# Keeping the numbers of a 1/rms iteration in free PSUM columns instead of in SBUF

## The chip, the cores and the metric

The kernel runs on one core of one Trainium2 chip. The metric is the device time of one execution in microseconds; 17 small VectorE instructions in each of four places are what changes.

## The reference, cut to what matters

The reference is an attention over 32 memory slots, followed by a gated feed-forward layer with an RMS norm in front (8 batches, 8 heads, 576 positions, head dimension 64, model width 512, inner width 1536, all fp32):

```python
x = attn_out.transpose(0, 2, 1, 3).reshape(B * S, H * D)   # 4608 x 512
rms = np.sqrt(np.mean(x * x, axis=-1, keepdims=True) + 1e-06)
xn = x / rms * rms_g
g = xn @ w_gate
silu = g * (1.0 / (1.0 + np.exp(-g)))
val = xn @ w_val
return (silu * val @ w_out).astype(np.float32)
```

The change concerns 1/rms alone: one number for each of the 4608 rows of x.

## The kernel before, in words

The batches are worked in four pairs, numbered 0 to 3. A pair has 1152 rows of x, held as 128 partitions by NT = 9 columns of row groups, so 1/rms of a pair is one tile of 128 x 9 floats, `rinv`. x itself is never formed: the kernel keeps the attention weights `a` and multiplies the weight matrices by the batch's memory values, and the sum of squares of a row is the weights times a Gram matrix times the weights again.

`x_steps` makes the steps for a pair. `turn` (line 184) transposes the attention weights on TensorE into `tp`, and `copy` (line 194) takes them to SBUF as `at`. `mm` (line 235) multiplies `at` by the Gram matrix `gb` into a PSUM tile `xp`, one for each of the nine groups; only its first 256 of 512 columns are used. `square` (line 248) multiplies `xp` by the weights and adds up each row into `ssq`. `fin` (lines 258 to 278) then computes 1/sqrt by a bit trick and four rounds of three instructions on VectorE: 17 instructions on 128 x 9 numbers, nearly all of which depend on the one before. `spread` transposes `rinv` on TensorE (`rp`, line 204), multiplies `at` by it on VectorE (line 212), and splits the product into a high and a low part: `ath` on ScalarE (line 223) and `atl` on GpSimd (line 224). The products of the feed-forward layer (lines 840, 876, 918) read these.

Pairs 0 and 1 pass through this in the first stage, together with the reductions of k and v (line 573 and its followers 588, 596, 597, 599, 605, 617, 642), the scores of the attention (lines 706, 717, 719, 726, 737 to 746) and the conversion of the weights from doubles in lines 345 to 403. There the PSUM tiles of `xp` come from a ring of two banks named "kx", which `kvp` and `kvt` use too. Pairs 2 and 3 pass through it in the second stage, beside the feed-forward products of pairs 0 and 1. There `xp`, the transposes and the output products `po` (line 918) share a ring of two banks named "o"; `po` is added to `acc` on VectorE (line 925), which frees its bank. Line 854 subtracts there the high part of a product from it, line 885 multiplies the two halves of the gate.

The order of the instructions is written out: every step has a date in a list (`ev`) from the constants in `PRM`, the list is sorted, and the steps are issued in that order; a scheduler then places each engine's instructions in a fixed order, by that priority and its own estimate of time, and gives out the banks of a ring. On the chip each engine works through its list and waits where an input or a bank isn't ready. Input transfers go through one queue, SP's.

Of the kernel before, what the change touches and what calls it, by code (L numbers as in the profile page):

```python
# [8 lines left out]
F32 = mybir.dt.float32  # L9
F32R = mybir.dt.float32r  # L10
I32 = mybir.dt.int32
U32 = mybir.dt.uint32
AF = mybir.ActivationFunctionType
ALU = mybir.AluOpType
# [76 lines left out]
def kernel(  # L91
# [25 lines left out]
    nc = tc.nc  # L117
    P = 128
# [3 lines left out]
    NT = S // 64  # L122
    NP = B // 2
    DM = H * D
# [7 lines left out]
    persist = ctx.enter_context(tc.tile_pool(name="persist", bufs=1))  # L132
# [9 lines left out]
    rinv = [persist.tile([P, NT], F32, name=f"rinv{i}") for i in range(NP)]  # L142
# [4 lines left out]
    ssqs = {}  # L147
# [14 lines left out]

    def x_steps(pr, a, psum_t, psum_x, fetch=None):

        tps, xps, srcs, st = {}, {}, {}, {}
        i = pr % G

        def first():
# [61 lines left out]
        def mm(t):  # L230
            def f():
                xps[t] = xp = psum_x(f"xp{pr}_{t}")
                for cc in range(2):
                    for j in range(2):
                        nc.tensor.matmul(  # L235
                            xp[64 * j:64 * j + 64, P * cc:P * cc + P],
                            st["at"][:, t, cc, 64 * j:64 * j + 64],
                            gb[:, j, cc],
                            start=True, stop=True,
                        )  # L240
            return f
# [13 lines left out]
            return f  # L255

        def fin():
            m = persist.tile([P, NT], F32, tag="m", name=f"m{pr}")
            nc.vector.tensor_scalar(
                out=m, in0=ssqs[pr], scalar1=0.0, scalar2=1.0 / DM, op0=ALU.max, op1=ALU.mult  # L260
            )
            nc.vector.tensor_scalar_add(m, m, 1e-6)
            r = rinv[pr]
            ri = r.bitcast(I32)
            nc.vector.tensor_scalar(
                out=ri, in0=m.bitcast(I32), scalar1=1, scalar2=None, op0=ALU.logical_shift_right
            )
            nc.vector.tensor_scalar(
                out=ri, in0=ri, scalar1=-1.0, scalar2=float(0x5F3759DF), op0=ALU.mult, op1=ALU.add
            )  # L270
            nc.vector.tensor_scalar(out=m, in0=m, scalar1=-0.5, scalar2=None, op0=ALU.mult)
            u = persist.tile([P, NT], F32, tag="u", name=f"u{pr}")
            for _ in range(4):
                nc.vector.tensor_tensor(out=u, in0=r, in1=r, op=ALU.mult)
                nc.vector.tensor_tensor(out=u, in0=u, in1=m, op=ALU.mult)
                nc.vector.scalar_tensor_tensor(
                    out=r, in0=u, scalar=1.5, in1=r, op0=ALU.add, op1=ALU.mult
                )
        events = [(-0.1, first)]
        for t in range(NT):  # L280
# [3 lines left out]
            if fetch and t % 4 == 0:  # L284
                events.append((t / 100 - 0.05, fetch(t)))
        p = NT + PRM["LAG"]
        events.append((p, fin))
        for t0, n in ((0, 4), (4, 4), (8, 1)):
            events += zip((p + PRM["RO"], p + PRM["RO"] + PRM["RS"], p + PRM["RO"] + 2 * PRM["RS"]), spread(t0, n))
# [138 lines left out]
    with ExitStack() as c1:  # L428
# [31 lines left out]
        st = {}  # L460
# [293 lines left out]
        def tile_of(tag):  # L754
            return lambda name: ps.tile([P, 512], F32, tag=tag, name=name, bufs=PRM["B"][0 if tag == "tr" else 1])
# [35 lines left out]
        for pr in range(G):  # L791
            for s in range(HP):
                t = PRM["S_AT"][pr * HP + s]
                steps = q_steps(pr, s)
                ev.append((t - PRM["QL"] - PRM["OL"] - PRM["QD"][pr * HP + s], lambda pr=pr, s=s: load_q(pr, s)))
                ev.append((t - PRM["QL"] - PRM["OL"], steps[0]))
                ev += place(t - PRM["QL"], PRM["QO"], steps[1:])
                ev += place(t, PRM["SO"], score_steps(pr, s))
            if pr < G:
                ev += [(PRM["X_AT"][pr] + PRM["XP"] * p, f) for p, f in x_steps(  # L800
                    pr, lambda t, pr=pr: a_tiles[pr][:, t], tile_of("tr"), tile_of("kx"))]
# [16 lines left out]
    def where(i):  # L818

        ps_, r = divmod(i, NU * G * 2)  # L820
        u, r = divmod(r, G * 2)
        pi, f = divmod(r, 2)
        return ps_, u, ps_ * G + pi, 2 * u + f
# [197 lines left out]
    def x2(pr):  # L1021
        got = {}

        def fetch(t):
            def f():
                for tag, t0, n in (("qr", 0, 4), ("qT", 4, 4), ("ex", 8, 1)):
                    if t0 == t:
                        a = sb.tile([P, n, 256], F32, tag=tag, name=f"ain{pr}_{t0}")
                        nc.sync.dma_start(a, a_dram[pr][:, t0:t0 + n])
                        for k in range(n):  # L1030
                            got[t0 + k] = a[:, k]
            return f
        steps = x_steps(pr, got.pop, o_tile, o_tile, fetch)
        return [f for _, f in steps]
# [7 lines left out]
    for i in range(NS):  # L1042
        ps_, u, pr, j = where(i)
# [62 lines left out]
```

## Time and the profile before

| | us |
|---|---|
| median of 3 runs | 908.46 (908.34 to 909.11) |
| the profiled execution | 907.8 |
| its span from first to last instruction | 906.0 |
| TensorE busy in matmuls | 837.0 (92%) |
| VectorE busy | 575.7 (64%) |
| ScalarE busy | 420.2 (46%) |
| GpSimd busy | 326.2 (36%) |

The page and the trace call the engines PE (TensorE matmul), PEld (TensorE weight load), DVE (VectorE), ACT (ScalarE), POOL (GpSimd) and SP (SyncE). L276 is line 276 of the kernel. `out<-in` names the tiles that an instruction writes and reads, then come partitions x elements and type. Idle time of an engine before an instruction stands behind it in square brackets, with what ended it. Shares over the whole span are averages of stages with different limits.

### The profile page before, as it was taken

Reading aid. Unit: us, or ns where it says so; the run is one execution under the profiler, and the core shown is the slowest. Engines: PE = TensorE matmul, PEld = TensorE weight load, DVE = VectorE, ACT = ScalarE, POOL = GpSimd, SP = SyncE. Lnnn points to the kernel's source line nnn. Section 1 sums busy time; section 2 is a strip of 40 time slices with the busy share of each in tenths; the row PEclk is TensorE's granted clock in tenths of the full one; section 3 lists DMA queues with packets and bytes.
Section 4 is the critical chain, followed back from the end, with each engine's and each line's share of the span. In section 5 each row is a group of like instructions: output and inputs, shape, how many; then the busy total and the mean of one; then the engine's idle time right before and its main releaser. Section 6 shows DMA issues by size and latency. Waiting matters only on the chain.

```text
span 906.0 us, 15847 instructions
## 1 busy us (share of the span) xinstructions
PE 837.0 (92%) x6207; PEld 744.5 (82%) x6207; DVE 575.7 (64%) x994; ACT 420.2 (46%) x717; POOL 326.2 (36%) x274
## 2 busy tenths in 40 slices
PE   4998485899998899999999999999999999999997
PEld 4776474788986798888898997799899999999996
DVE  5577959896788777877855656532445455454543
ACT  2666334787765355664642443254424333233330
POOL 3464735553636245344532331411212121121120
PEclk9899787999999999999999999999999999999999
DMA  8986554454445332543413133501204013040046
GB/s 277 337 278 209 201 166 120 168 146 107 164 133 162 101 119 84 152 114 103 140 57 129 52 88 118 121 31 47 94 1 140 1 47 93 1 140 1 1 114 142
DMA packets 81506, 106.41 MB, mean 117 GB/s; under 512 B 34324, under 2 KB 52248, under 8 KB 81432
## 3 DMA queue, kind: packets, MB, share of 16 engines
q1 hardware_dynamic: 81432, 105.41, 37.6%
q8 instruction: 49, 0.80, 0.4%
q14 instruction: 25, 0.20, 0.1%
HBM read 73.93 MB, written 31.46 MB: 116 GB/s over the span
## 4 chain that ended last, share of the span: by engine, by line
PE 73%; DVE 14%; DMA 4%; ACT 3%; issue 3%; POOL 2%; SPq 1%; POOLq 0%; ACTq 0%; DVEq 0%
PE po L918 30%; PE pv L876 15%; PE pg L876 15%; PE vp L840 7%; DMA phi<-in_phi_dram 2%; PE xp L235 2%; DVE mi L365 1%; DVE mi L369 1%; DVE xl L854 1%; DVE ex L345 1%; PE kvp L573 1%; DMA q<-in_q_dram 1%; DVE ex L347 1%; DVE acc L925 1%; SPq L298 1%
## 5 line engine op out<-in xcount | busy, mean ns | idle before, releaser
L899 POOL TENSOR_TENSOR hl<-hf,hh 128x512 fp32r<-128x512 f32 (+1 forms) x96 | 139.8, 1457 | 361.3 <-ACT hh L898 353.3
L925 DVE TENSOR_TENSOR acc<-po,acc 128x512 f32<-128x512 f32 x180 | 123.0, 687 | 128.0 <-PE po L918 127.2
L918 PE MATMUL po<-oh,hh 128*128 128x512 f32 x432 | 173.5, 403 | 8.3 <-DVE acc L925 5.2
L918 PE MATMUL po<-oh,hl 128*128 128x512 f32 x432 | 171.3, 397 | 0.0
L918 PE MATMUL po<-ol,hh 128*128 128x512 f32 x432 | 171.0, 396 | 0.0
L884 ACT ACTIVATE sg<-pg 128x256 f32<-128x256 f32 x192 | 78.2, 409 | 171.2 <-PE pg L876 150.0
L854 DVE TENSOR_TENSOR xl<-vp,xh 64x1024 fp32r<-64x1024 f32 x96 | 117.1, 1220 | 48.1 <-ACT xh L853 47.0
L885 DVE TENSOR_TENSOR hf<-pv,sg 128x256 f32<-128x256 f32 x192 | 85.5, 453 | 79.1 <-PE pv L876 51.6
L853 ACT CAST xh<-vp 64x1024 fp32r<-64x1024 f32 x96 | 96.6, 1007 | 53.6 <-PE vp L840 25.5
L918 PEld LDWEIGHTS po<-oh,hh 128*128 128x128 f32 x432 | 81.5, 189 | 23.5 <-DVE acc L925 7.5
L898 ACT CAST hh<-hf 128x512 fp32r<-128x512 f32 (+1 forms) x96 | 64.6, 673 | 77.0 <-DVE hf L885 54.2
L918 PEld LDWEIGHTS po<-oh,hl 128*128 128x128 f32 x432 | 81.4, 189 | 19.4
L876 PE MATMUL pg<-ath,xh 128*128 128x320 f32 (+1 forms) x384 | 86.6, 300 | 8.5 <-ACT xh L853 6.0
L918 PEld LDWEIGHTS po<-ol,hh 128*128 128x128 f32 x432 | 81.7, 189 | 11.1
L840 PE MATMUL vp<-wh,vm 128*128 128x256 f32 x384 | 86.9, 289 | 3.5 <-DVE at L212 2.3
L876 PE MATMUL pv<-ath,xh 128*128 128x320 f32 (+1 forms) x384 | 84.8, 300 | 3.2 <-DVE hf L885 3.1
L876 PE MATMUL pg<-atl,xh 128*128 128x320 f32 (+1 forms) x384 | 85.0, 297 | 0.0
L876 PE MATMUL pg<-ath,xl 128*128 128x320 f32 (+1 forms) x384 | 84.8, 295 | 0.0
L876 PE MATMUL pv<-atl,xh 128*128 128x320 f32 (+1 forms) x384 | 84.5, 297 | 0.0
L876 PE MATMUL pv<-ath,xl 128*128 128x320 f32 (+1 forms) x384 | 84.1, 297 | 0.0
L876 PEld LDWEIGHTS pg<-ath,xh 128*128 128x128 f32 x384 | 63.6, 191 | 14.1 <-ACT xh L853 6.6
L840 PEld LDWEIGHTS vp<-wh,vm 128*128 128x128 f32 x384 | 66.8, 193 | 6.2 <-DVE at L212 2.5
(129 smaller groups left out, 1394.6 us busy)
## 6 DMA issues: line engine op xcount, KB each, us to landing
kv<-in_k_dram SPq DMA_DIRECT2D x32, 288.0 KB, 5.0
kv<-in_v_dram SPq DMA_DIRECT2D x32, 288.0 KB, 5.6
out_dram<-acc SPq DMA_DIRECT2D x72, 128.0 KB, 2.4
raw<-in_moe_w_gate_dram SPq DMA_DIRECT2D x12, 512.0 KB, 3.9
raw<-in_moe_w_val_dram SPq DMA_DIRECT2D x12, 512.0 KB, 3.7
wd<-wh SPq DMA_DIRECT2D x12, 512.0 KB, 3.0
wd<-wl SPq DMA_DIRECT2D x12, 512.0 KB, 4.5
raw<-in_moe_w_out_dram SPq DMA_DIRECT2D x12, 512.0 KB, 3.5
```

The costliest lines, as they stand in the source:

```text
L235: nc.tensor.matmul(xp[64 * j:64 * j + 64, P * cc:P * cc + P], st["at"][:, t, cc, 64 * j:64 * j + 64], gb[:, j, cc], start=True, stop=True,)
L298: issued.append(nc.sync.dma_start(out, in_).ins)
L840: nc.tensor.matmul(vp[:, cc, e, :], lhs(l), r[:, 2 * cc + e, :], start=(n == 0), stop=(n == 2),)
L853: nc.scalar.copy(xh[rows], src)
L854: nc.vector.tensor_tensor(out=xl[rows], in0=src, in1=xh[rows].bitcast(F32), op=ALU.subtract)
L876: nc.tensor.matmul(pt[:, :N], l[:, cc, b, half * P:half * P + P], r[:, b, cc, t0:t0 + n, :].rearrange("p t x -> p (t x)"), start=(m == 0), ...
L884: nc.scalar.activation(sg[:, :N], pg[:, :N], AF.Silu)
L885: nc.vector.tensor_tensor(out=hf[:, :, b, :], in0=pv[:, :N].rearrange("p (t x) -> p t x", x=64), in1=sg[:, :N].rearrange("p (t x) -> p t x ...
L898: nc.scalar.copy(hh, hv)
L899: nc.gpsimd.tensor_tensor(out=hl, in0=hv, in1=hh.bitcast(F32), op=ALU.subtract)
L918: nc.tensor.matmul(po, l[:, tt, :], r, start=(m == 0), stop=(m == 5))
L925: nc.vector.tensor_tensor(out=accs[key], in0=po, in1=accs[key], op=ALU.add)
```

## The change

In `fin`, the numbers m and r of the iteration move from SBUF tiles into two stretches of nine columns (256 to 264 and 272 to 280) of the PSUM tile of the pair's last `xp`; m is written back to SBUF by the instruction that multiplies it by -0.5, u stays in SBUF, and the last instruction writes `rinv` in SBUF as before. The product that was r*r, then times m, is now r*m, then times r. The count of instructions is the same. The last `xp` is now used until the iteration's last instruction.

```diff
--- before.py
+++ after.py
@@ -162,7 +162,7 @@
 
     def x_steps(pr, a, psum_t, psum_x, fetch=None):
 
-        tps, xps, srcs, st = {}, {}, {}, {}
+        tps, xps, srcs, st, xlast = {}, {}, {}, {}, []
         i = pr % G
 
         def first():
@@ -230,6 +230,7 @@
         def mm(t):
             def f():
                 xps[t] = xp = psum_x(f"xp{pr}_{t}")
+                xlast[:] = [xp]
                 for cc in range(2):
                     for j in range(2):
                         nc.tensor.matmul(
@@ -255,26 +256,26 @@
             return f
 
         def fin():
-            m = persist.tile([P, NT], F32, tag="m", name=f"m{pr}")
+
+            mp, rp = (xlast[0][:, 256 + 16 * k:256 + 16 * k + NT] for k in range(2))
+            m, u = (persist.tile([P, NT], F32, tag=x, name=f"{x}{pr}") for x in "mu")
             nc.vector.tensor_scalar(
-                out=m, in0=ssqs[pr], scalar1=0.0, scalar2=1.0 / DM, op0=ALU.max, op1=ALU.mult
+                out=mp, in0=ssqs[pr], scalar1=0.0, scalar2=1.0 / DM, op0=ALU.max, op1=ALU.mult
             )
-            nc.vector.tensor_scalar_add(m, m, 1e-6)
-            r = rinv[pr]
-            ri = r.bitcast(I32)
+            nc.vector.tensor_scalar_add(mp, mp, 1e-6)
+            ri = rp.bitcast(I32)
             nc.vector.tensor_scalar(
-                out=ri, in0=m.bitcast(I32), scalar1=1, scalar2=None, op0=ALU.logical_shift_right
+                out=ri, in0=mp.bitcast(I32), scalar1=1, scalar2=None, op0=ALU.logical_shift_right
             )
             nc.vector.tensor_scalar(
                 out=ri, in0=ri, scalar1=-1.0, scalar2=float(0x5F3759DF), op0=ALU.mult, op1=ALU.add
             )
-            nc.vector.tensor_scalar(out=m, in0=m, scalar1=-0.5, scalar2=None, op0=ALU.mult)
-            u = persist.tile([P, NT], F32, tag="u", name=f"u{pr}")
-            for _ in range(4):
-                nc.vector.tensor_tensor(out=u, in0=r, in1=r, op=ALU.mult)
-                nc.vector.tensor_tensor(out=u, in0=u, in1=m, op=ALU.mult)
+            nc.vector.tensor_scalar(out=m, in0=mp, scalar1=-0.5, scalar2=None, op0=ALU.mult)
+            for k in range(4):
+                nc.vector.tensor_tensor(out=u, in0=rp, in1=m, op=ALU.mult)
+                nc.vector.tensor_tensor(out=u, in0=rp, in1=u, op=ALU.mult)
                 nc.vector.scalar_tensor_tensor(
-                    out=r, in0=u, scalar=1.5, in1=r, op0=ALU.add, op1=ALU.mult
+                    out=rinv[pr] if k == 3 else rp, in0=u, scalar=1.5, in1=rp, op0=ALU.add, op1=ALU.mult
                 )
         events = [(-0.1, first)]
         for t in range(NT):
```

## Rows read from the trace of the kernel before

**Rows 1.** Table of stages: us from:to, length, busy us and instructions of each engine, PEclk, DMA share, GB/s.
```profile
91.00:104.00 13.00, 6.86 (x135) 6.51 (x136) 12.63 (x32) 3.83 (x8) 8.23 (x11) 0.90 0.69 233
104.00:117.00 13.00, 7.95 (x75) 6.85 (x75) 12.58 (x23) 5.07 (x11) 10.01 (x10) 0.58 0.33 122
122.00:128.00 6.00, 4.93 (x40) 3.79 (x38) 0.98 (x4) 2.30 (x6) 3.20 (x4) 0.73 1.01 349
499.00:517.00 18.00, 18.00 (x115) 16.09 (x114) 11.42 (x31) 6.92 (x12) 3.86 (x3) 1.00 0.06 15
```

**Rows 2.** Waits from 85 to 155 us: who for whom, us in total, times, longest.
```profile
PE rp L204 <- DVE rinv L276: 7.6, 2, 5.6
```

**Rows 3.** Order of time on VectorE, pair 0: start us, us, engine, line, operation.
```profile
93.03 1.12 DVE L259 TENSOR_SCALAR m<-ssq 128x9 f32<-128x9 f32 x1
...
94.72 0.90 DVE L347 TENSOR_SCALAR ex<-ex 128x512 int32<-128x512 int32 x1
...
97.97 0.66 DVE L275 TENSOR_TENSOR u<-u,m 128x9 f32<-128x9 f32 x1
98.66 1.18 DVE L276 SCALAR_TENSOR_TENSOR rinv<-u,rinv 128x9 f32<-128x9 f32 x1
99.88 0.41 DVE L274 TENSOR_TENSOR u<-rinv 128x9 f32<-128x9 f32 x1
...
100.75 1.19 DVE L274 TENSOR_TENSOR u<-rinv 128x9 f32<-128x9 f32 x1
...
103.33 0.16 DVE L276 SCALAR_TENSOR_TENSOR rinv<-u,rinv 128x9 f32<-128x9 f32 x1
```

**Rows 4.** Order of time on GpSimd, beside pair 0.
```profile
94.08 1.26 POOL L403 TENSOR_TENSOR wl<-w,wh 128x512 fp32r<-128x512 f32 x1
97.77 0.83 POOL L737 TENSOR_TENSOR half<-ex 128x288 f32<-128x288 f32 x1 [2.42 <-DVE rinv L268]
98.56 1.25 POOL L385 TENSOR_TENSOR w<-mi,ex 128x512 f32<-128x512 f32 x1
...
100.65 1.26 POOL L403 TENSOR_TENSOR wl<-w,wh 128x512 fp32r<-128x512 f32 x1
```

**Rows 5.** Order of time on VectorE, pair 1.
```profile
136.25 0.17 DVE L259 TENSOR_SCALAR m<-ssq 128x9 f32<-128x9 f32 x1
...
138.11 1.23 DVE L276 SCALAR_TENSOR_TENSOR rinv<-u,rinv 128x9 f32<-128x9 f32 x1
```

**Rows 6.** Order of time on GpSimd, beside pair 1.
```profile
138.05 1.26 POOL L403 TENSOR_TENSOR wl<-w,wh 128x512 fp32r<-128x512 f32 x1 [10.94 <-PE kvp L573]
```

**Rows 7.** VectorE's groups by shape, 85 to 155 us: count, busy us, mean ns, idle before.
```profile
L248 DVE CUSTOM_DVE_ANT_0 xp<-xp,a 128x256 f32<-128x256 f32 x13 | 5.5, 435 | 4.5 <-PE xp L235 4.4
...
L719 DVE TENSOR_TENSOR ex<-S,mxs 128x576 f32<-128x576 f32 x3 | 2.3, 754 | 0.0
...
L605 DVE TENSOR_TENSOR kb<-kvp,im 128x256 f32<-128x256 f32 x3 | 1.2, 400 | 0.1
...
L597 DVE RECIPROCAL si<-si 128x2 f32<-128x2 f32 x3 | 0.5, 161 | 0.0
...
L596 DVE TENSOR_SCALAR si<-kvp 128x2 f32<-128x2 f32 x3 | 0.5, 154 | 1.6 <-PE kvp L588 1.6
```

**Rows 8.** The page's costliest groups: busy us, mean ns, idle before, releaser.
```profile
L925 DVE TENSOR_TENSOR acc<-po,acc 128x512 f32<-128x512 f32 x180 | 123.0, 687 | 128.0 <-PE po L918 127.2
...
L854 DVE TENSOR_TENSOR xl<-vp,xh 64x1024 fp32r<-64x1024 f32 x96 | 117.1, 1220 | 48.1 <-ACT xh L853 47.0
```

**Rows 9.** Order of time on TensorE, pair 3.
```profile
562.74 0.50 PE L918 MATMUL po<-oh,hh 128*128 128x512 f32 x1
...
564.25 0.39 PE L918 MATMUL po<-oh,hh 128*128 128x512 f32 x1
...
572.30 1.04 PE L204 MATMUL rp<-ident,rinv 128*128 128x128 f32 x4 [2.26 <-DVE rinv L276]
```

**Rows 10.** Order of time on VectorE, pair 3.
```profile
568.64 1.09 DVE L275 TENSOR_TENSOR u<-u,m 128x9 f32<-128x9 f32 x1
```

## The prediction

> **What bounds the kernel now.** I began with the table of stages: it shows which engine fills each stretch. From 91 to 117 us VectorE is the full one (12.63 of 13 us, then 12.58 of 13), while TensorE is busy for 6.86 and 7.95 us of it; from 499 to 517 us TensorE works 18.00 of 18.00 us [rows 1]. So the four runs of the iteration do not stand in the same surroundings. Pairs 0 and 1 (from 93 and 136 us [rows 3, 5]) lie where VectorE sets the pace, pairs 2 and 3 (after 500 and 560 us) lie beside TensorE work. The list of waits between 85 and 155 us confirms the first half: TensorE waits twice for line 276, the iteration's last line, 7.6 us together and 5.6 us the longer [rows 2]. I then read the order of time on VectorE through the iteration of pair 0, with GpSimd's beside it.
>
> There the reader is to see two things. A free instruction on nine columns takes 0.16 to 0.17 us, but in pair 0 some take 0.41 to 1.19 us [rows 3]. And the longest three of the dependent ones end where a GpSimd instruction ends: line 276, from 98.66 to 99.84, against GpSimd's line 385 until 99.82; line 274, from 100.75 to 101.94, against line 403 until 101.91; line 275, until 98.63, against line 737 until 98.56 [rows 3, 4]. They did not work, they waited for GpSimd. In pair 1 one instruction does the same: 138.11 to 139.34, while GpSimd's line 403 runs from 138.05 to 139.31 [rows 5, 6].
>
> Which instructions wait? The ones held in rows 3 and 5 read two SBUF operands, or are a tensor_scalar from SBUF to SBUF. Those with one operand in PSUM do not: line 248 (PSUM and SBUF in, PSUM out) means 435 ns over 13 instructions and line 719 means 754 ns over 3, in the same crowded stretch [rows 7]. That is the row on which the forecast stands.
>
> **The change, part by part.** The count stays: 17 VectorE instructions for each of four pairs, 68 in all. No transfer, matmul or ScalarE instruction is added. What differs is operands and how long one PSUM bank is held.
>
> *a. Two SBUF operands become one.* Lines 274 to 276 read rp from PSUM and one SBUF operand each. The first five work on mp and rp; only the first of them still reads SBUF. If they behave as line 248, the holds go.
> Pair 0, with 0.17 as the free duration [rows 3]: line 275 0.66 - 0.17 = 0.49; line 276 1.18 - 0.17 = 1.01; line 274 0.41 - 0.17 = 0.24 and 1.19 - 0.17 = 1.02. Sum 2.76 us. Line 259 took 1.12 too, but I count nothing for it: if it shrank, line 347 (tensor_scalar, SBUF) would come 0.95 earlier and sit out the same GpSimd instruction, which starts at 94.08 and lasts until 95.34; line 347 already ends only at 95.62 [rows 3, 4]. So 2.76 is the figure, with 0 below it, if later SBUF instructions take over the hold, and 3.7 above.
> Pair 1: 1.23 - 0.17 = 1.06 us [rows 5].
> Does it reach the end? After pair 0 VectorE stays full until 117, and its next instructions read PSUM (717, 719, 596, 212). I take all of it. The transfers that saturate from 122 to 128 us (DMA share 1.01) [rows 1] were issued only when that VectorE work let the queue go on, so they move along; the other view is a rival below. After pair 1 lines 212, 223 and 224 follow directly and the pairs' first products wait for them.
>
> *b. The price of a PSUM operand on nine columns.* The trace has no chain that writes PSUM and reads it back. Nearest rows: line 596 reads PSUM and takes 154 ns for 128x2, line 597 reads SBUF and takes 161 ns, so -7 ns; line 248 reads and writes PSUM, 435 ns, against 400 for line 605, which writes SBUF, so +35 ns [rows 7]. Bounds -0.1 to +0.6 us for 17 instructions. I take 0, since the durations of 596 and 597 are those of our size.
> [...]
>
> *c. Order inside the iteration.* Before, u = r*r needed only r; line 271 (m times -0.5) ran beside line 268. Now u = rp*m needs both, and both touch one bank. Consecutive dependent instructions start 0.21 us apart (9 such steps in 1.86 us from 136.25 to 138.11 [rows 5]), so at most one such step more, and about 0.1 if the two still overlap: I take +0.15 for each pair, 0.3 on the path for pairs 0 and 1 (bounds 0 and 0.42).
>
> *d. The bank of the last xp is held until the iteration ends.* In pairs 0 and 1 the ring is "kx" with two banks. After xp of pair 0 the next user takes the bank of the one before it, and the following one (line 617) needs line 605's output first, which comes after the iteration. The same order holds in pair 1. Cost 0, bounds 0 and about 0.5.
> In pairs 2 and 3 the ring is "o", two banks, through which the output products of line 918 pass. With one bank left, each waits for line 925 of the one before, 687 ns [rows 8], and its hand-over, about 0.9 us, unless other products stand between. Pair 2: most have others between; I count one short stall, 0.3 us (bounds 0 and 0.9). Pair 3: four such products run in a row from 562.74 us, 1.5 us each (the second starts at 564.25 [rows 9]), so three stalls, 2.7 us; but TensorE then idles 2.26 us at 572.30 for the iteration's result anyway [rows 9], and line 275 there loses its hold, 1.09 - 0.17 = 0.92 [rows 10]. If the VectorE order stays, the later 925s push the end of the iteration out by 2.7 - 0.92 = 1.8; if two of them move behind it, it ends 0.92 + 2 x 0.69 = 2.3 earlier, about the idle time that there is to win. I take 0 between them.
>
> **Sum.** -2.76 - 1.06 + 0.3 + 0.3 + 0 = -3.2 us. The profiled execution takes 907.8 (span 906.0, 1.8 around it), so 904.6; the median of the runs shown, 908.46, is 0.66 above that execution: 905.3 us.
>
> **Rivals.**
> 1. *The wait only moves.* GpSimd stays as busy, and a later SBUF instruction (lines 744, 345) takes over pair 0's hold, or the transfers before 128 us do not come earlier. For it: DMA share 1.01 from 122 to 128 [rows 1]. Against: only 0.33 before it, so that burst was late issued rather than a backlog. Left: pair 1's 1.06 less 0.15 and pair 2's 0.3: -0.6, 907.8 us.
> 2. *A PSUM operand costs.* At the upper bound of 35 ns [rows 7], 17 instructions cost 0.6 us in each of pairs 0, 1 and 3: -3.2 + 1.8 = -1.4, 907.1 us. It eats all at about 0.1 us an instruction in pairs 0 and 1 (3.2 / 34). [...]
> 3. *The held bank blocks the output products (slower).* If the next user of the "o" ring is bound to the held bank instead of the free one, the second product after the last xp waits until the iteration ends. Pair 2: at least 3.6 us (the iteration takes 17 x 0.21 = 3.6). Pair 3: 3.6 plus an interleaved line 854, 1.2 us, and line 925, 0.7 [rows 8], 5.5, less the idle 2.26: 3.3. Together 6.9 against the gain of 3.8 - 0.3: +3.4, 911.9 us. It decides from stalls of 3.5 us on. For it: TensorE has no slack at 499 to 517 [rows 1]. Against: each ring has a free bank at that moment, and there are other products to put there.
> 4. *The change doesn't act:* the holds stay although an operand is in PSUM: 908.5. Line 248 and 719 speak against it; small.
>
> **How the numbers follow.** Forecast 0.53; rival 1 0.15, rival 2 0.14, rival 3 0.14, rival 4 0.04. A measurement of this kernel tells about 0.2% from no change, 1.8 us, so same is 906.6 to 910.3. The forecast's own range, from the bounds of a to d and pair 3's -2.3 to +1.8, is 902.4 to 907.4; about a tenth of it is inside "same". Rivals 1, 2 and 4 lie in "same" (a quarter of rival 2 is faster); rival 3 is slower in most of its span, and a changed order of work adds a little to slower. Faster 0.55, same 0.28, slower 0.17. Leaving out rival 3 and the far ends, 8 in 10 lie between 902.4 and 909.0.
>
> **What the profile after would show.** Step a: no instruction of the iteration over 0.25 us in pairs 0 and 1 (line 259 perhaps), and TensorE's 5.6 us wait for line 276 near 2.9. Step b: free durations within 0.03 of 0.17, starts 0.21 apart. Step c: line 271 a step after 268. Step d: TensorE's idle time before line 918 under 1 us at 500 to 517, and its idle time before line 204 in pair 3 below 2.26. Also the first products of line 876, after 154 us, some 3.5 us earlier. Wrong would be: starts over 0.3 apart (rival 2), line 918 waiting for line 276 (rival 3), the same date of the first line 876 products (rival 1), or another order of instructions that moves the whole middle of the kernel.

## The result and the profile after

The changed kernel takes 912.8 us (median of 6 runs, 910.21 to 914.93), the kernel before 908.4 beside it: ratio 1.005, 95% interval 1.003 to 1.0069. That is 4.5 us slower (0.005 x 908.4), where 3.2 us faster was forecast. A second series of the same program, in the experiments below, gave 1.0036 (1.0019 to 1.0054), 3.3 us. Both intervals lie above 1; the two figures, 4.5 and 3.3 us, are each known to about 1.7 us either way.

Where the time goes is not where the change is. The iteration itself did what the forecast said. This is the order of time of the profile after, on VectorE and then on GpSimd, through pair 0; it answers to [rows 3, 4]. In the changed file the iteration stands in lines 262 to 277; every line from 233 on has moved down by one or more.

```profile
92.79 0.15 DVE L262 TENSOR_SCALAR xp<-ssq 128x9 f32<-128x9 f32 x1
...
93.52 0.64 DVE L348 TENSOR_SCALAR ex<-ex 128x512 int32<-128x512 int32 x1
94.08 1.77 DVE L370 SCALAR_TENSOR_TENSOR mi<-raw,mi 128x512 f32<-128x512 uint32 x1
...
97.38 0.17 DVE L273 TENSOR_SCALAR m<-xp 128x9 f32<-128x9 f32 x1
97.58 0.17 DVE L275 TENSOR_TENSOR u<-xp,m 128x9 f32<-128x9 f32 x1
97.78 0.17 DVE L276 TENSOR_TENSOR u<-xp,u 128x9 f32<-128x9 f32 x1
97.99 0.17 DVE L277 SCALAR_TENSOR_TENSOR xp<-u,xp 128x9 f32<-128x9 f32 x1
98.19 0.17 DVE L275 TENSOR_TENSOR u<-xp,m 128x9 f32<-128x9 f32 x1
...
101.02 0.17 DVE L277 SCALAR_TENSOR_TENSOR rinv<-u,xp 128x9 f32<-128x9 f32 x1
...
93.84 1.46 POOL L404 TENSOR_TENSOR wl<-w,wh 128x512 fp32r<-128x512 f32 x1
...
98.14 1.26 POOL L386 TENSOR_TENSOR w<-mi,ex 128x512 f32<-128x512 f32 x1
```

GpSimd's line 386 runs from 98.14 to 99.40, and six instructions of the iteration start and end beside it, each 0.17 us long, 0.20 to 0.21 apart. Before, the like took 1.18 and 1.19 us [rows 3]. One hold has moved: line 370 of the weights' conversion reads two SBUF operands and now sits out GpSimd's line 404 (94.08 to 95.85 against 93.84 to 95.30). Before, line 259 had been held (1.12 us) and line 369, the same step, took 0.68. The forecast counted this part as no gain, but expected line 347 to be the one held; that step (348 now) takes 0.64. The groups by line and shape over the whole span, with busy us and mean ns, say the same of all four pairs:

```profile
L276 DVE TENSOR_TENSOR u<-xp,u 128x9 f32<-128x9 f32 x16 | 2.7, 168 | 0.4
L275 DVE TENSOR_TENSOR u<-xp,m 128x9 f32<-128x9 f32 x16 | 2.7, 167 | 0.4
L277 DVE SCALAR_TENSOR_TENSOR xp<-u,xp 128x9 f32<-128x9 f32 x12 | 2.1, 171 | 0.3
...
L262 DVE TENSOR_SCALAR xp<-ssq 128x9 f32<-128x9 f32 x4 | 0.6, 156 | 0.0
```

TensorE's waits from 85 to 155 us answer to [rows 2]. No rp product waits for the iteration's last line any more, which had cost 7.6 us in two places; the longest wait of an rp product is 3.6 us instead of 5.6. The 1.9 us for line 277 are line 618's, the next user of a bank of "kx" in pair 1. Its inputs are ready at 134.48 and 134.81 and the iteration ends at 134.88, so the held bank adds 0.4 us at most.

```profile
PE pg L877 <- ACT xh L854: 4.4, 1, 4.4
PE rp L204 <- DVE si L598: 3.6, 1, 3.6
...
PE kvt L618 <- DVE rinv L277: 1.9, 1, 1.9
```

The loss comes later, and it is seen best by the same instruction in both traces. Line 854 (855 after) runs 96 times, spread over the feed-forward stages. The table gives by how many us its k-th run starts later in the changed kernel's profiled execution; the head is its date in the kernel before. (The profiled execution of after took 910.21, span 908.4; it is the fastest of the six runs, so this trace shows 2.6 us less than the median run takes.)

| date before | 152 | 185 | 212 | 240 | 266 | 310 | 500 | 543 | 589 | 865 |
|---|---|---|---|---|---|---|---|---|---|---|
| after | -6.7 | -6.7 | -3.5 | -1.2 | +3.6 | +3.9 | +4.0 | +4.0 | +3.1 | +2.6 |

The first stage ends 6.7 us earlier. Between 185 and 266 us 10.3 of it are lost, and 0.3 more by 310, in a stretch without any instruction of the iteration. Part of the lead at 185 is work put off: 20 matmuls that the old order does before that run of line 854 come after it in the new one, while at 152 and at 310 the counts agree. The stages of pairs 2 and 3, where a PSUM bank is held longer, change little.

What differs there is the order of the work. The instructions are the same ones, but the scheduler, which places them by its own estimate of time, gave every engine another list: the lists of the two kernels agree up to pair 0's iteration, and from there they differ in three places: the rest of the first stage, the start of the second stage (up to some 300 us), and pairs 2 and 3. Here is what the new list does in the middle, in order of time on VectorE, GpSimd, ScalarE and TensorE:

```profile
247.55 1.50 DVE L346 TENSOR_SCALAR ex<-raw 128x512 int32<-128x512 int32 x1 [1.50 <-POOL w L386]
248.96 1.77 DVE L366 TENSOR_SCALAR mi<-raw 128x512 int32<-128x512 int32 x1
250.66 1.48 DVE L348 TENSOR_SCALAR ex<-ex 128x512 int32<-128x512 int32 x1
252.06 1.75 DVE L370 SCALAR_TENSOR_TENSOR mi<-raw,mi 128x512 f32<-128x512 uint32 x1
...
246.22 1.30 POOL L386 TENSOR_TENSOR w<-mi,ex 128x512 f32<-128x512 f32 x1 [2.11 <-ACT mi L377]
247.47 2.98 POOL L900 TENSOR_TENSOR hl<-hf,hh 128x512 fp32r<-128x512 f32 x2
250.42 2.84 POOL L404 TENSOR_TENSOR ol<-w,oh 128x512 fp32r<-128x512 f32 x2
...
252.23 0.63 ACT L351 ACTIVATE ex<-ex 128x512 int32<-128x512 int32 x1 [3.18 <-DVE ex L348]
252.77 0.57 ACT L971 COPY qT<-qtp 128x512 f32<-128x512 f32 x1
...
253.39 0.50 PE L919 MATMUL po<-oh,hh 128*128 128x512 f32 x1 [3.31 <-ACT qT L971]
254.87 0.80 PE L877 MATMUL pv<-ath,xh 128*128 128x256 f32 x2 [0.98 <-DVE hf L886]
```

These are holds like the ones that the change took out of the iteration. Four conversion steps with SBUF operands take 1.48 to 1.77 us each while GpSimd works from 246.22 to 253.26 without a gap; the round before, at 242.19, took 0.43, 0.42, 1.52 and 0.68. The holds themselves are not new: of the 95 conversion steps on VectorE between 152 and 310 us, 14 take over 1.4 us in the kernel before and 15 after. In the kernel before these three come at almost the same date, and TensorE has no wait from 211 to 270 us:

```profile
244.54 1.44 DVE L347 TENSOR_SCALAR ex<-ex 128x512 int32<-128x512 int32 x1
245.90 2.06 DVE L369 SCALAR_TENSOR_TENSOR mi<-raw,mi 128x512 f32<-128x512 uint32 x1
247.88 1.77 DVE L358 SCALAR_TENSOR_TENSOR ex<-raw,ex 128x512 int32<-128x512 int32 x1
```

New is what stands behind them. After the change ScalarE's line 351 waits 3.18 us for one of the held steps, the copy qT stands behind it in ScalarE's list, and TensorE waits 3.31 us for qT. The table of stages (columns as in [rows 1]) shows what follows in these 16 us:

```profile
250.00:254.00 4.00, 0.58 (x2) 0.19 (x1) 4.00 (x4) 1.20 (x3) 3.26 (x3) 1.00 0.17 62
254.00:258.00 4.00, 3.13 (x12) 2.96 (x13) 2.22 (x4) 3.25 (x6) 2.83 (x2) 0.51 0.49 147
258.00:262.00 4.00, 4.00 (x20) 3.68 (x19) 2.60 (x8) 2.29 (x4) 0.00 (x0) 0.64 0.43 145
262.00:266.00 4.00, 4.00 (x40) 3.46 (x38) 3.76 (x6) 1.40 (x3) 1.19 (x1) 1.00 0.58 127
```

After the idle stretch the granted clock of TensorE is 0.51 and then 0.64, and 12 and 20 matmuls pass in four microseconds where 40 pass at 262. The clock is not the same in every execution: in the trace of experiment 11, the same order again, waits of 3.32 and 0.98 us at this place are followed by 0.63 and 0.94.

### The profile page after: what moved, and what is told of

Read it like the earlier page. It is cut to its first block, busy times and chain, and to the rows that moved or that the text cites. A ratio compares the mean times of both kernels' runs of the same rounds, so it can differ in the third digit from the quotient of the medians.

```text
span 908.4 us, 15837 instructions
## 1 busy us (share of the span) xinstructions
PE 842.7 (93%) x6207; PEld 748.1 (82%) x6207; DVE 572.4 (63%) x994; ACT 420.6 (46%) x717; POOL 325.1 (36%) x274
## 4 chain that ended last, share of the span: by engine, by line
PE 75%; DVE 14%; DMA 4%; issue 3%; ACT 2%; POOL 2%; SPq 0%; POOLq 0%; DVEq 0%; ACTq 0%
PE po L919 30%; PE pv L877 15%; PE pg L877 14%; PE vp L841 7%; PE kvp L574 3%; DVE mi L370 2%; PE xp L236 2%; DMA phi<-in_phi_dram 2%; DVE xl L855 1%; DVE ex L346 1%; DVE mi L366 1%; DVE ex L348 1%; POOL w L386 1%; DMA kv<-in_v_dram 1%; DVE ex L359 1%
```

## The experiments

The theories. **P**, the plan: the new order of instructions costs more than the operands give. **R**, the arrival: the second stage comes earlier and collides with transfers and conversions. **H**, the held bank: the longer use of the last xp's bank costs what the holds gave.

To tell order and operands apart, kernels were made in which each engine's order is written down. Every pinned kernel has this edit, on the changed kernel or on the kernel before; ORDER holds the list of each engine, taken from the one or the other up to a cut. It adds no instruction, and no cost of it is seen: experiment 11, the changed kernel with its own order pinned, has a ratio of 1.0036, inside the interval of the changed kernel itself.

```diff
+def pin_order(nc, tc):
+    traced = list(nc.cur_bb.bb.instructions)
+    by = {i.name: i for i in traced}
...
+    for seq in json.loads(zlib.decompress(base64.b85decode(ORDER))):
+        prev = None
+        for n in seq:
+            i = squares[-n - 1] if n < 0 else by[f"I-{n}"]
+            if prev is not None:
+                tc.add_manual_dep(i, prev.name, mybir.DependencyInfo(
+                    mybir.DependencyClass.NoSync, mybir.DependencyReason.DATA))
+            prev = i
...
         tile_mem_attention_swiglu_kernel(tc, *args)
+        pin_order(nc, tc)
```

The cuts are one place in the issue order of all engines. On VectorE the first, called "158 us" in the expectations, falls at 134 us in the trace of after (at 151 to 157 on the other engines), since the engines do not stand at the same date; "188 us" and "300 us" are named by VectorE and by the end of the differing stretch.

**1. The changed operands in the order of the kernel before.** The edit above on the changed kernel, ORDER from the kernel before.

> The changed kernel, with every engine's instructions pinned to the order that the kernel before has. Nothing is left out. Theory P (the plan): on each instruction the change does what it was to do, and its loss comes from another fixed order of work in the second stage, which the planner wrote because it thinks the iteration takes another time. Then this runs at 902 to 906 us, 3 to 6 below the kernel before. Theory R (arrival): the second stage is paced by the conversion and transfer of the weights; coming to it earlier gains nothing and the waits only move. Then 909 to 913, whatever the order. Theory H (held bank): the bank of the last xp blocks the output products of pairs 2 and 3. Then above 908.4, with TensorE idle before line 919 between 500 and 580 us.

Measured: 906.92 us (12 runs), ratio 0.998 (0.9965 to 0.9995), so 1.8 us faster, just above the 902 to 906 us of P. Nothing is lost in the middle:

| date before | 152 | 185 | 212 | 240 | 266 | 310 | 500 | 543 | 589 | 865 |
|---|---|---|---|---|---|---|---|---|---|---|
| experiment 1 | -1.4 | -1.6 | -1.6 | -1.6 | -1.6 | -1.6 | -1.6 | -1.1 | -0.3 | +0.5 |

With the same order the terms can be read one by one. Pair 0's iteration takes from 95.07 to 102.81, 7.74 us, against 93.03 to 103.49, 10.46 [rows 3]: 2.72 less. Pair 1's takes from 135.75 to 139.20, 3.45, against 136.25 to 140.57, 4.32 (its first instruction [rows 5]; its last starts at 140.40 and takes 0.17): 0.87 less. Then 1.3 us are given back at pairs 2 and 3 (-1.6 to -0.3). The start of pair 0's iteration is 2 us late in this execution (95.07 against 93.03), in a stretch that the change doesn't touch; single executions differ by such amounts, which is why sizes are taken from the ratios and places from the dates. In the fourteen traces this start lies between 92.16 and 95.75 us, though the lists ahead of it are the same. Dates of two executions therefore compare better when they are counted from it. Counted so, the run of line 854 at 152 us comes after:

| | before | 1 | 7 | 6 | 5 | 3 | 10 | after | 11 |
|---|---|---|---|---|---|---|---|---|---|
| order of the first stage | old | old | old | new | new | new | new | new | new |
| iteration of pairs 0 and 1 | SBUF | PSUM | PSUM | SBUF | PSUM | PSUM | PSUM | PSUM | PSUM |
| us from pair 0's first instruction | 59.0 | 55.6 | 56.0 | 56.0 | 52.7 | 52.8 | 52.4 | 52.5 | 52.9 |

(Experiments 3 to 10 are described below.) In the old order the operands give 3.4 and 3.0 us, close to the 3.59 that the iterations lost in length; in the new order 3.2 to 3.6 (5, 3 and 10 against 6). R falls as the cause of the loss: an arrival 1.6 us earlier stays 1.6 us for 350 us, and in experiment 5, which is 6.4 us early at 185, it stays 6.4 to 310.

**2. The kernel before in the order of the changed kernel.** The same edit on the kernel before, ORDER from the changed kernel; the iteration stays in SBUF.

> The kernel before (iteration in SBUF), with every engine's instructions pinned to the order of the changed kernel. Nothing is left out. Theory P: the order alone carries the loss and the gain on the instructions is missing: 914 to 918 us. Theory R: the order does not matter and the early arrival is gone: 907.5 to 909.5. Theory H: no bank is held here, so 908 to 909.

Measured: 914.54 us (6 runs), ratio 1.0073 (1.0053 to 1.0094), 6.6 us slower. No operand has changed here and no bank is held longer, so the order alone costs as much as the change lost, or more. H falls as the main cause. The same stall stands in the trace, 3.33 us for qT at 259.79.

**3 and 4. The order of the middle, both ways.** Experiment 3 is the changed kernel in its own order, with the middle (from the cut at 134 us to some 300 us) in the order of the kernel before; experiment 4 is the kernel before in its own order, with the middle in the changed kernel's.

> The changed kernel in its own order, except that the middle (from about 158 to about 300 us, the first products of the second stage) is pinned to the order of the kernel before. Nothing is left out. Theory P: the 10 us that the changed kernel loses between 195 and 260 us are gone: 901 to 905. Theory R: 910 to 914, as the changed kernel. Theory H: 910 to 914, since pairs 2 and 3 are as in the changed kernel.

> The kernel before in its own order, except that the middle (from about 158 to about 300 us) is pinned to the order of the changed kernel. Nothing is left out. Theory P: slower, 913 to 918, by an order that no instruction of the iteration stands in. Theory R: 907.5 to 909.5, since nothing arrives earlier. Theory H: 908 to 909.

Measured: experiment 3 takes 900.37 us (6 runs), ratio 0.991 (0.9891 to 0.993), 8.2 us faster than the kernel before; experiment 4 takes 919.61, ratio 1.0124 (1.0102 to 1.0146), 11.3 us slower, more than the 913 to 918 us expected. So the new order of the middle costs 11 us with the old operands, and 11 to 13 with the new ones (1.0036 or 1.005 less 0.991, of 908.5). In experiment 4 the dates go from +3.5 at 185 to +15.6 at 310. P holds, and its place is the middle.

**5 and 6. What the first stage's order and the operands are worth apart.** Both have the changed kernel's order in the first stage and the old one from there to the end; experiment 5 with the changed operands, experiment 6 with the iteration in SBUF.

> The changed kernel with its own order of instructions up to about 158 us, and from there to the end the order of the kernel before (e3_change_old_middle went back to its own order after about 300 us). Theory P (the order of work decides more than the operands): e3 gained 1.6 us after 495 us, from -4.2 to -5.8 against the kernel before, and e1_change_old_order, with the old order there, lost 2.1 (-1.6 to +0.5). If that is the order of the end, this kernel takes 900.4 + 3.7 = 904 us. Rival (the end's order does not matter, the two differ by the noise of a run): 900.4 within 1.5.

> The kernel before with its iteration in SBUF, in exactly the order of e5_change_old_middle_and_end: the changed kernel's order up to about 158 us, its own order after. The difference to e5 is the worth of the operands alone. Steps a to d of the forecast: e5 is 3.2 us faster than this one. If the better time of e3 came from the changed kernel's order of the first stage and not from the operands (theory P in its strong form), this one equals e5 within 1 us. Rival (the held bank costs what the holds gave): this one is no slower than e5, and faster at the end.

Measured: 903.08, ratio 0.9949 (0.993 to 0.9969), and 904.49, ratio 0.9956 (0.9934 to 0.9978). The new order of the first stage gives 4.0 us with the old operands (1 - 0.9956), 3.0 by the table of experiment 1. Between 5 and 6 the operands as a whole can't be told from nothing (0.0007, with intervals of 0.004). The traces say why: up to 152 us experiment 5 is 3.3 us quicker than 6 (52.7 against 56.0), and between 500 and 589 us 5 loses 1.2 while 6 gains 1.4. So what the operands give in pairs 0 and 1 the held bank takes in pairs 2 and 3. (Bare dates mislead here: at 185 us 5 stands at -6.4 and 6 at -4.5, but 3, the same program as 5 up to some 495 us, at -4.2.) Experiment 5 against 3 (0.9949, 0.991) says that the end's new order is better as well, by 3.5 us in the ratios and by 2.7 in the dates after 500 us (3: -4.1 to -5.8; 5: -6.3 to -5.3).

**7. The held bank by itself.** Experiment 1, with the iteration of pairs 2 and 3 put back into SBUF.

```diff
+        def fin_sbuf():
+            m = persist.tile([P, NT], F32, tag="m", name=f"m{pr}")
...
+        if pr >= 2:
+            fin = fin_sbuf
```

> e1_change_old_order (the changed iteration in the order of the kernel before) with the iteration of pairs 2 and 3 put back into SBUF, as before; pairs 0 and 1 stay in PSUM. So no bank of the ring o is held, the order is the same. Forecast (step d about 0): 906.9, as e1, within 1 us. Theory H (the held bank delays the output products, and that is where e1 lost 2.1 us after 495 us): 904.8. In its profile the three waits of line 919 for line 926 in pair 3 (0.78 us each in e1) are gone, and the hold of line 276 there (1.09) is back.

Measured: 903.82 us (10 runs), ratio 0.9955 (0.9939 to 0.997), 4.1 us faster than the kernel before, and 2.3 faster than experiment 1 by the ratios; by the dates, from 500 to 589 us, 1.4 (it goes from -1.5 to -1.6 there, experiment 1 went from -1.6 to -0.3). The waits of TensorE from 495 to 592 us show the bank. First experiment 1:

```profile
PE po L919 <- DVE acc L926: 2.6, 4, 0.8
PE rp L204 <- DVE rinv L277: 1.3, 1, 1.3
```

Then experiment 7, in which the added lines move 277 to 300:

```profile
PE rp L204 <- DVE rinv L300: 2.3, 1, 2.3
```

Three of the four waits stand in pair 3, one behind the other, in experiment 1's order of time on TensorE:

```profile
564.10 0.50 PE L919 MATMUL po<-oh,hh 128*128 128x512 f32 x1 [0.78 <-DVE acc L926]
...
566.55 0.50 PE L919 MATMUL po<-oh,hh 128*128 128x512 f32 x1 [0.78 <-DVE acc L926]
...
569.02 0.50 PE L919 MATMUL po<-oh,hh 128*128 128x512 f32 x1 [0.78 <-DVE acc L926]
...
573.38 0.65 PE L204 MATMUL rp<-ident,rinv 128*128 128x128 f32 x4 [1.26 <-DVE rinv L277]
```

With one bank left, a product waits until the one before it has been added to acc. The wait for rinv falls from 2.26 [rows 9] to 1.26, and 2.6 - 1.0 = 1.6 is the price in waits. The hold that was expected back is there, 1.09 us, on the line that was 275.

Every trace can be read in this way, since all of them pass the stretch between the same two runs of line 854, at 500 and 589 us, in one of four kinds:

| order there | iteration of pairs 2 and 3 | traces | length, us | TensorE idle | granted clock |
|---|---|---|---|---|---|
| old | SBUF | before, 4, 7 | 88.99 to 89.10 | 3.1 | 0.98 |
| old | SBUF | 6, 8 | 87.70 to 87.72 | 3.1 | 1.00 |
| old | PSUM | 1, 5 | 90.36 | 4.7 | 1.00 |
| new | SBUF | 2, 10 | 87.05 to 87.06 | 2.7 | 1.00 |
| new | PSUM | after, 3, 9, 11, 12 | 88.10 to 88.15 | 3.2 | 1.00 |

H is right in the small. In the old order the bank costs 2.7 us where the clock is 1.00 on both sides, and 1.3 against the traces in which it fell after the wait for rinv (in before, after 2.26 us of it, to 0.53 from 572.3 to 574.0 us and 0.54 from there to 576.0). In the changed kernel's own order it costs 1.1.

**8. An edit without a price.** In the kernel before, line 271 is written ahead of line 268. Nothing is pinned.

```diff
+            nc.vector.tensor_scalar(out=m, in0=m, scalar1=-0.5, scalar2=None, op0=ALU.mult)
             nc.vector.tensor_scalar(
                 out=ri, in0=ri, scalar1=-1.0, scalar2=float(0x5F3759DF), op0=ALU.mult, op1=ALU.add
             )
-            nc.vector.tensor_scalar(out=m, in0=m, scalar1=-0.5, scalar2=None, op0=ALU.mult)
```

> The kernel before with line 271 (m times -0.5) written ahead of line 268 (the second step of the bit trick): the same 17 instructions on the same SBUF tiles, nothing pinned, so the scheduler plans anew. Theory P: an edit with no price of its own changes the fixed order of work elsewhere too, and the time moves by 1 to 5 us in either direction. Rival (only the change of operands re-plans the middle; such a swap is neutral): 908.5 within 0.9.

Measured: 906.78 us (12 runs, 902.49 to 911.11), ratio 0.9978 (0.9957 to 0.9998). The lists do change elsewhere: compared place by place in the traces, some 90 of TensorE's matmuls and 34 of ScalarE's instructions stand otherwise, where the change gave some 750 and 140. The time moves by 2.0 us, barely told from nothing. It goes with P, but it is weak: a small edit re-planned little and moved the time little.

**9 and 11. Four instructions moved in the new middle.** Experiment 11 is the changed kernel with its own order pinned, as a measure. Experiment 9 moves four instructions of it, in this order of the lists:

```diff
 ScalarE
+L971 qT
+L885 sg
 L351 ex
-L971 qT
 L377 mi
-L885 sg
 VectorE
 L346 ex
+L886 hf
 L366 mi
+L886 hf
 L348 ex
 L370 mi
 L359 ex
-L886 hf
-L886 hf
```

> The changed kernel in its own order throughout, with four instructions moved in the middle, around 250 us: on ScalarE one copy qT (line 971) and one sg (line 885) go ahead of a conversion step (line 351) that waited there 3.18 us for VectorE; on VectorE two hf (line 886) go in between the five conversion steps (lines 346 to 370) that GpSimd held up, instead of behind them. Theory P, made local (TensorE's 3.3 us wait for qT and 1.0 us wait for hf, and the half granted clock after them, 0.51 and 0.64 in the 8 us from 254 to 262, come from that queue order): the waits at 253.4 and 254.9 shrink by 3 us or more, the clock stays 1.00, and the time falls by 3 to 6 us against e11_change_own_order. Rival (the conversions are the bottleneck, the wait comes back within some 20 us): less than 1 us.

> The changed kernel with every engine's order written down and pinned as its own scheduler gave it: the same program as the changed kernel, as a measure beside e9_change_four_moved. All theories: 912.8, 1.005 of the kernel before, within 0.2%.

Measured: 910.37 (12 runs), ratio 1.0007 (0.9995 to 1.0019), and for experiment 11 912.63 (12 runs), ratio 1.0036 (1.0019 to 1.0054). So the four moves give back 2.6 us by the ratios (0.0029 x 908.8; with these intervals, between 0.7 and 4.5), less than the three to six expected, and more than the rival's one. TensorE's waits at that place, in experiment 9:

```profile
253.03 0.50 PE L877 MATMUL pv<-ath,xh 128*128 128x256 f32 x2 [0.74 <-DVE hf L886]
257.26 0.33 PE L965 MATMUL qtp<-ident,qr 128*128 128x128 f32 x1 [1.49 <-ACT qT L971]
```

The 3.31 and 0.98 have become 0.74 and 1.49, the clock stays at 1.00 in all of 250 to 266 us, and against the profile of after the dates go from +2.0 at 239 to -0.6 at 270: 2.6 us won there. Against the trace of experiment 11 they win only 1.3 from 240 to 269, and lose 1.7 again by 311; the granted clock from 270 to 300 us is 1.00 there and 0.94 here. TensorE's idle time from the run at 240 to the run at 269 us is 2.9 us in experiment 9 against 4.3 in both others, but up to the run at 310 it is 9.4 against 9.7 in after and 10.6 in 11: the stall is gone, but only 0.3 to 1.2 us of the idle time stay won, so a part of the wait comes back, as the rival had it. That the moves are worth 2.6 us, about a quarter of what the middle loses, rests on the ratios; between single traces (72.7 us from 240 to 310, against 75.2 in after and 72.3 in 11) the clock decides more. This kernel is faster than the changed one and still not faster than the one before.

**12. A shorter stretch put back.** Experiment 3 with the cut at 188 us instead of 134.

> e3_change_old_middle with a shorter stretch put back: the changed kernel in its own order up to about 188 us (VectorE's line 348 there) and from about 300 us on, and the order of the kernel before only in between; e3 goes back already from 134 us on VectorE. Theory P, made local (what the new order loses lies between 185 and 285 us, where the changed kernel falls from 6.7 us ahead to 4.0 behind): 0.991 to 0.993 of the kernel before, as e3, about 901 us. Rival (the loss is prepared between 134 and 188 us, where the new order sends the conversions of the weights and the first products off differently, and comes out later): 1.000 or above.

Measured: 905.84 us (5 runs), ratio 0.996 (0.9946 to 0.9975), halfway between both expectations. The dates split the loss:

| date before | 152 | 185 | 212 | 240 | 266 | 310 | 500 |
|---|---|---|---|---|---|---|---|
| after | -6.7 | -6.7 | -3.5 | -1.2 | +3.6 | +3.9 | +4.0 |
| experiment 3 | -4.2 | -4.2 | -4.2 | -4.2 | -4.2 | -4.2 | -4.1 |
| experiment 12 | -5.4 | -5.4 | -1.1 | -1.1 | -1.1 | -0.2 | -0.5 |

Experiment 12 loses 4.3 us up to 212, as the changed kernel does there (3.2; the 20 matmuls put off past 185 are in both), and from then on keeps what it has, where the changed kernel loses 7 more. By the ratios the order from 188 us on costs 0.9960 against 1.0036 or 1.005, 7 to 8 us, and the order between 134 and 188 us 0.991 against 0.996, 4.5 us. What each single move of the second part costs beside the four of experiment 9 stays open.

**10. The best of them.** Experiment 3 with the iteration of pairs 2 and 3 in SBUF, as in experiment 7.

> e3_change_old_middle (0.991 of the kernel before) with the iteration of pairs 2 and 3 put back into SBUF, in the same order of instructions. Theory H in its small form (the held bank costs 1.3 us in pairs 2 and 3 with the old order there, e1 against e7_change_pairs_0_1_only): with this order, in which e2_old_operands_new_order gained 3.5 us after 495 us and the changed kernel 1.4, it saves about 2 us, 0.989 of the kernel before. Rival (in this order the output products have room, the held bank costs nothing): as e3, 0.991, or slower by the hold that comes back in pair 3.

Measured: 900.04 us (6 runs), ratio 0.9905 (0.9883 to 0.9927), 8.6 us faster than the kernel before. Against experiment 3 (0.991) the runs don't tell; the waits for line 926 (951 here) fall from 1.9 us to 0.3 from 495 to 592 us, and the stretch from 500 to 589 takes 87.1 us instead of 88.1. Both beat both kernels. Most of that is the plan: the new order in the first stage and at the end, the old one between.

## Why the prediction was wrong

*The step that failed* is none of a to d but the sum's premise, "What differs is operands and how long one PSUM bank is held": it priced the 68 instructions and one bank and put the order of all the others at nothing, without a reason. The prediction named "another order of instructions that moves the whole middle of the kernel" only in its last sentence, as what would make it wrong, with no price and hardly a chance ("a changed order of work adds a little to slower"). The description of the kernel ahead of it says that the scheduler places the instructions by its own estimate of time, so it had to be expected that an edit of an operand's place in memory could change the plan. The runs show in its place: order alone, +6.6 us (experiment 2), of which the first stage -4.0 (6), the middle +11.3 (4), and the end between -0.7 (the rest of experiment 2) and -3.5 (3 against 5).

*Step a*, two SBUF operands become one: right, in mechanism and size. No instruction of the iteration is over 0.17 us in pairs 0 and 1. Pair 0 lost 2.72 and pair 1 0.87 us in the same order, 3.59 together; a and c of these pairs had been put at -2.76 - 1.06 + 0.30 = -3.52. TensorE's 5.6 us wait for line 276, forecast near 2.9, is 2.9 in experiments 1 and 7. Line 259's hold was rightly counted as nothing, though line 370 took it over and not 348 (347 before). That the gain reaches the end is shown too, by experiment 7: -4.1 us (-5.5 to -2.7).

*Step b*, the price of a PSUM operand: right, 0. The chain that writes PSUM and reads it back starts every 0.20 to 0.21 us, as the one in SBUF did [rows 5]. The durations are the same too: the means are 156 to 171 ns for PSUM operands against 0.16 to 0.17 us before.

*Step c*, one step more: as told; line 273 starts 0.19 to 0.21 us after line 270, and pair 1's 3.45 us in experiment 1 are 0.19 more than 4.32 - 1.06, where 0.15 was taken.

*Step d*, the held bank: the mechanism was right, three stalls in pair 3 and a short one in pair 2, 0.78 us each where 0.9 was reckoned, and 0.2 where 0.3. The hand-over in the 0.9 was the author's estimate, about 0.2 us; in experiment 1 it is 0.09, 0.78 less the 0.69 of line 926. The balance was mis-sized. The forecast set the end of pair 3 at 0 between -2.3 and +1.8 because the wait for the iteration would be eaten up; in the old order that wait fell only from 2.26 to 1.26. In place of +0.3 the step costs 1.3 to 2.7 us there and 1.1 in the changed kernel's own order. With that size the sum is -3.6 + 1.1 + 6.6 = +4.1, and the change measured +4.5 and +3.3; the measured terms are each known to about 2 us, so the agreement is better than it had to be. The range stated, 902.4 to 907.4, is also narrower than the bounds of a to d, which added up at their ends reach from about 901 to 913.

*The rivals.* Rival 1 (the wait only moves) fell: in the old order the first products of line 876 come 57.9 and 58.3 us after pair 0's first instruction (experiments 1 and 7) instead of 61.3, where 3.5 us sooner was said, and both keep the gain. (In the changed kernel's own order they come at 147.63 instead of 154.30, but about half of that is the order.) Rival 2 fell with step b. Rival 3 gave the right sign for a wrong reason: no product of line 919 waits for line 277 in any of these traces, and without the new order the held bank leaves a gain. Rival 4 fell with step a.

*What the middle loses, as far as it is shown.* Between the runs of line 854 at 152 and 310 us the kernel before, the changed one and experiment 11 have the same 991 matmuls. In the table of stages, first before, then after, then experiment 11 (the order of after in another execution):

```profile
152.00:309.90 157.90, 141.97 (x991) 128.34 (x992) 129.04 (x200) 105.63 (x178) 80.12 (x59) 0.97 0.49 150
```

```profile
145.30:313.80 168.50, 148.55 (x991) 133.54 (x992) 131.33 (x200) 106.17 (x178) 79.52 (x60) 0.93 0.45 137
```

```profile
145.70:311.30 165.60, 145.13 (x991) 130.42 (x992) 132.73 (x200) 106.13 (x178) 79.75 (x60) 0.96 0.46 139
```

After takes 10.6 us more. TensorE idles 15.9 us before and 20.0 after, 4.0 more; the other 6.6 are the same matmuls taking longer, at a granted clock of 0.93 instead of 0.97. In experiment 11 it is 7.7 us more, 4.5 of them idle and 3.2 in longer matmuls, at 0.96. So the waits of the new order cost 4.0 to 4.5 us in both, and what the clock adds differs from one execution to the next. Which waits they are is only read from the traces; the one that experiment 9 removed came back in part.

## What to carry to other kernels

Where a scheduler fixes the order by its own estimate, an edit of a few instructions is two changes, the operands and the plan; compare the two lists before a time is forecast or explained, and price the edit with the order held. In this kernel the plan was worth up to 11 us, three times the edit, and the fastest version (which the runs don't tell from experiment 3) took the new operands only in the pairs that hold no contended bank. A hold seen at one place (a VectorE instruction on SBUF operands alone beside a busy GpSimd, 1.18 us in place of 0.16 [rows 3]) is worth looking for at every place with the same kind of instruction: here four conversion steps of 1.5 to 1.8 us, no rarer in the kernel before, stopped TensorE only where the new plan had put a copy that it needed behind one of them in ScalarE's list.

## What was not expected of the hardware

A VectorE chain of 128 x 9 that writes PSUM and reads it back ran at the same pace as one in SBUF, 0.20 to 0.21 us from start to start, and even the instruction that goes from SBUF to PSUM (line 262, mean 156 ns) was not held in any of the four pairs, where line 259, SBUF to SBUF, had taken 1.12 us [rows 3]. And a TensorE wait was followed by a stretch at a lower clock: after the 3.31 us at 253.4 and the 0.98 behind it the granted clock was 0.51 and 0.64 for eight microseconds (0.63 and 0.94 in experiment 11 after 3.32 and 0.98), while in experiment 9 it stayed at 1.00 after waits of 0.74 and 1.49 at the same place.
